# A decode step's last product: two column groups in two PSUM banks, copied by two engines, with the residual added by matmul

## The chip, the core and the metric

The kernel runs on one core of a Trainium2 chip. The metric is the device time of one launch in microseconds (us), the median of several runs. One further execution was recorded by the hardware profiler; its views are quoted here. PE is TensorE, PEld its weight loads, DVE VectorE, ACT ScalarE, POOL GpSimd and SP SyncE. L548 is line 548 of the kernel before.

## The reference

A decode step of one transformer block, batch 4, one new token, width 1024, bf16 inputs:

```python
x = A_x                                            # 4 x 1 x 1024
h = x + attention(layernorm(x), k_cache, v_cache, wq, wo)
#   q = layernorm(x) @ wq: 32 heads of 128; 4 KV heads; the last 2048 of 8192 cached rows
#   scores = q k^T * 128**-0.5; softmax; times v; @ wo (4096 x 1024)
h2 = h + (silu(n @ w1) * (n @ w3)) @ w2            # n = layernorm(h); w1, w3: 1024 x 3584; w2: 3584 x 1024
return h2                                          # 4 x 1 x 1024, bf16
```

## The kernel before

All weights and the used part of the caches pass once through one large SBUF buffer, `ring`, of five units. SP issues these loads in a fixed order (`load`, L123): wq in three pieces, K by batch entry, V, then wo, w1, w3, and w2 in five pieces of 13, 8, 4, 2 and 1 rows of 128 x 1024 (`W2B`, L114). A load waits until the part of the ring that it overwrites has been read. The order of instructions on each engine is that of the program (`manual_schedule`, L130).

The four batch entries are padded to 32 rows (R = 32), so a product of 4 x 1024 takes four column groups of the PE array: group c writes the PSUM partitions 32c to 32c+31 and holds columns 256c to 256c+255 (DQ = 256, C = 4). The stage that matters is the last:

- `h1` (L479) holds x + attention in float32, 128 x 256, in that layout of four groups.
- `hg_T` (L519) is the transposed product of silu(gate) and up, the stationary operand of the last product.
- The first two pieces of w2 (21 rows) go into `early_ps` (L533), two column groups of 512 columns each, 64 partitions by two banks. VectorE adds `early_ps` into `h1` (L544), half by half.
- The last three pieces (4, 2 and 1 rows) go into `y2_ps`, a part of the PSUM tile `small` (L548): for each row four matmuls of 256 columns, one in each of the four column groups, all in one bank.
- VectorE adds `h1` to `y2_ps` and writes `res` as bf16 (L558). Four stores of 4 rows by 512 bytes take it to the output: two on SP's queue, two on ACT's (L562).

`layernorm_T` (L187) and `up_projection` (L487) come ahead of this; the pieces of w2 are issued at L508 while the gate is computed. ACT's last work before the stores is the exponential of the gate and an addition (L511, L512). `ident_f` (L149) is a float32 identity of 128 x 128.

Of the kernel before, what the change touches and what calls it, by code (L numbers as in the profile page):

```python
# [10 lines left out]
P = 128  # L11
ACT = mybir.ActivationFunctionType
ALU = mybir.AluOpType
AX = mybir.AxisListType
BF16 = mybir.dt.bfloat16
FP32 = mybir.dt.float32
# [5 lines left out]
def kernel(  # L22
# [20 lines left out]
    nc = tc.nc  # L43

    B, _, D = A_x.shape
# [7 lines left out]
    FC = F // P  # L53
    NK = W // P
    C = 4
    R = 32
    S = R // B
    DQ = D // C
# [7 lines left out]
    x_flat = A_x.flatten_outer_dims()  # L66
    out_flat = out.flatten_outer_dims()
# [16 lines left out]
    const = ctx.enter_context(tc.tile_pool(name="const", bufs=1))  # L84
    act = ctx.enter_context(tc.tile_pool(name="act", bufs=1))
# [3 lines left out]
    ps = ctx.enter_context(tc.tile_pool(name="ps", bufs=1, space=bass.MemoryType.PSUM))  # L89
# [33 lines left out]
    def load(dst, src):  # L123
        nc.sync.dma_start(out=dst, in_=src)
# [6 lines left out]


    x_nat = act.tile([P, DQ], BF16)
    nc.gpsimd.memset(x_nat[:], 0.0)
    nc.scalar.dma_start(out=x_nat[::S, :], in_=x_flat.rearrange("b (c n) -> c b n", c=C))
    for r in (slice(0, 1), slice(1, KC // 2), slice(KC // 2, KC)):
        load(wq_s[:, r, :], wq_v[:, r, :])
    for b in range(B):
# [10 lines left out]
    ident_f = const.tile([P, P], FP32)  # L149
# [8 lines left out]
        out=same[:], in_=t32[:].rearrange("p (o h) -> p o h", o=1).to_broadcast([P, C, R])  # L158
    )
    gmask = const.tile([P, 1, Hkv], BF16)  # L160
    with nc.allow_low_precision("sums of zeros and a single one"):
        nc.vector.tensor_reduce(
            out=gmask[:, 0], in_=t32[:].rearrange("p (g r) -> p g r", g=Hkv), axis=AX.X, op=ALU.add
# [3 lines left out]
    for j in range(JM):  # L167
# [3 lines left out]
        out=nscale[:], in_=ident_f[:2, :2], scalar=-qscale, op=ALU.mult  # L171
# [5 lines left out]
        out=place[:, : R * C].rearrange("p (h e) -> p h e", e=C)[:, :, C - 1], in_=t32[:]  # L177
# [6 lines left out]
        out=gather[:, :, :B], in_=ident[:].rearrange("p (c b s) -> p c b s", c=C, b=B)[:, :, :, 0]  # L184
# [44 lines left out]
    for kc in range(KC):  # L229
        for hf in range(2):  # L230
            for c in range(C):
# [3 lines left out]
                    lhsT=xn_T[:, kc, :],  # L235
                    rhs=wq_s[:, kc, o : o + HALF * Dh],
                    start=(kc == 0),
                    stop=(kc == KC - 1),
                    tile_position=(0, R * c),
# [5 lines left out]
    for r in range(REP):  # L245
# [8 lines left out]
        out=Qm[:].rearrange("p b (g y) -> p b g y", y=QW)[:, :, :, :REP],  # L254
        in_=qT_ps[:, :, :, :B].rearrange("p r g b -> p b g r"),
# [72 lines left out]
    def softmax(b):  # L328

        p1 = act.tile([P, W // C], BF16, tag=("hg", "eg")[b % 2], name="p1")  # L330
        nc.scalar.activation(  # L331
            out=p1[:],
            in_=sc_ps[b // 2][:, b % 2],
            func=ACT.Exp,
            bias=stage[("bias", b // 2)][:, b % 2 : b % 2 + 1],
            scale=qscale,
            accum_out=rs[:, b : b + 1],
        )
        stage[("p1", b)] = p1

    def spread(b):

        P4 = ktpool.tile([P, JR * L5, Hkv], BF16, tag="P4")
        nc.vector.tensor_tensor(  # L344
            out=P4[:],
            in0=stage.pop(("p1", b))[:].rearrange("p (x o) -> p x o", o=1).to_broadcast([P, JR * L5, Hkv]),
            in1=gmask[:].to_broadcast([P, JR * L5, Hkv]),
            op=ALU.mult,
        )
        stage[("P4", b)] = P4  # L350
# [13 lines left out]
    def transpose_p(b):  # L364
        PT = ptpool.tile([P, JR, R], BF16, tag="PT")
        nc.vector.transpose(  # L366
            out=PT[:].rearrange("p j h -> p (j h)"),
            in_=stage.pop(("P4", b))[:].rearrange("p x g -> p (x g)"),
        )
        stage[("PT", b)] = PT  # L370


    def output(b):
        PT = stage.pop(("PT", b))
        o_ps = (
            small[:, 0].rearrange("p (j d) -> p j d", j=JM)
            if b % 2
            else ps.tile([P, JM, Dh], FP32, tag="ktA", name="o_ps")[:]
        )
        for i in range(JR // JM):  # L380
            nc.tensor.matmul(  # L381
                o_ps,
                lhsT=PT[:, i * JM : (i + 1) * JM, :].rearrange("p j h -> p (j h)"),
                rhs=v_s[b][:, i * JM : (i + 1) * JM, :],
                start=(i == 0),
                stop=(i == JR // JM - 1),
            )
        od = act.tile([P, JM, Dh], FP32, tag="od", bufs=1)
        nc.vector.scalar_tensor_tensor(  # L389
            out=od[:],  # L390
            in0=o_ps,
            scalar=rinv[:, b : b + 1],
            in1=jmask[:].to_broadcast([P, JM, Dh]),
            op0=ALU.mult,
            op1=ALU.mult,
        )
        o2 = act.tile([P, 2, Dh], FP32, tag="o2", bufs=1)
        nc.gpsimd.tensor_tensor(out=o2[:], in0=od[:, :2], in1=od[:, 2:], op=ALU.add)  # L398
        nc.gpsimd.tensor_tensor(out=om[:, b], in0=o2[:, 0], in1=o2[:, 1], op=ALU.add)
# [10 lines left out]
    small = ps.tile([P, 2, 512], FP32, tag="ktB")  # L410
# [11 lines left out]
    bias_of(1)  # L422
    softmax(2)
    softmax(3)
    spread(1)
    transpose_p(1)
    total(0)
# [2 lines left out]
    transpose_p(2)  # L430
    output(1)
    load(w1_s, w1_v)
    spread(3)
    transpose_p(3)
    total(1)
# [4 lines left out]
    for e in range(C):  # L440
        nc.tensor.matmul(
            on_ps[:],
            lhsT=place[:, C - 1 - e : C - 1 - e + P],
            rhs=om[:, :, e * T : (e + 1) * T],
            start=(e == 0),
            stop=(e == C - 1),
# [6 lines left out]
    for i in range(2):  # L453
        for k in range(2):
            c = i + 2 * k
            nc.tensor.matmul(
                y_ps[R * i : R * i + R, k],
                lhsT=gather[:, c, :],
                rhs=x_nat[:],
                start=(k == 0),  # L460
                stop=False,
                tile_position=(0, R * i),
                skip_group_check=True,
            )
    for t in range(T):
        row = wo_s[:, t].rearrange("p (k i n) -> p i k n", k=2, i=2)
        for i in range(2):
            nc.tensor.matmul(  # L468
                y_ps[R * i : R * i + R],
                lhsT=oP[:, t, :],  # L470
                rhs=row[:, i],
                start=False,
                stop=(t == T - 1),
                tile_position=(0, R * i),
                skip_group_check=True,
            )
    load(w3_s, w3_v)
    load(w2_s[0], w2_v[:, : W2B[0], :])
    h1 = act.tile([P, DQ], FP32)  # L479
    for k in range(2):  # L480
        nc.vector.tensor_copy(out=h1[2 * R * k : 2 * R * k + 2 * R, :], in_=y_ps[:, k])
# [25 lines left out]
    fc = W2B[0]  # L507
    for w, n in zip(w2_s[1:], W2B[1:]):  # L508
# [8 lines left out]
        out=hg[:].rearrange("p (a f) -> p a f", a=2), in0=up_ps[:, :, :FH], in1=eg[:], op=ALU.mult  # L517
    )
    hg_T = act.tile([P, FC, R], BF16)  # L519
# [1 line left out]


    early_ps = ps.tile([2 * R, 2, DQ], FP32, tag="ktA", name="early_ps")
    y2_ps = small[:, 0, :DQ]
    NE = 2
    FE = sum(W2B[:NE])

    fc = 0
    for w, n in zip(w2_s[:NE], W2B[:NE]):
        for ff in range(n):  # L530
            row = w[:, ff].rearrange("p (k i n) -> p i k n", k=2, i=2)
            for i in range(2):
                nc.tensor.matmul(  # L533
                    early_ps[R * i : R * i + R],
                    lhsT=hg_T[:, fc, :],
                    rhs=row[:, i],
                    start=(fc == 0),
                    stop=(fc == FE - 1),
                    tile_position=(0, R * i),
                )  # L540
            fc += 1
    for k in range(2):
        part = h1[2 * R * k : 2 * R * k + 2 * R, :]
        nc.vector.tensor_tensor(out=part, in0=early_ps[:, k], in1=part, op=ALU.add)  # L544
    for w, n in zip(w2_s[NE:], W2B[NE:]):
        for ff in range(n):
            for c in range(C):
                nc.tensor.matmul(  # L548
                    y2_ps[R * c : R * c + R, :],
                    lhsT=hg_T[:, fc, :],  # L550
                    rhs=w[:, ff, c * DQ : (c + 1) * DQ],
                    start=(fc == FE),
                    stop=(fc == FC - 1),
                    tile_position=(0, R * c),
                )
            fc += 1
    res = act.tile([P, DQ], BF16)
    nc.vector.tensor_tensor(out=res[:], in0=y2_ps[:], in1=h1[:], op=ALU.add)  # L558
    for i in range(2):
        for half, eng in enumerate((nc.sync, nc.scalar)):  # L560
            c = 2 * half + i
            eng.dma_start(  # L562
                out=out_flat[:, c * DQ : (c + 1) * DQ], in_=res[R * c : R * c + B, :]
            )


# [28 lines left out]
```

## Time and profile before

| what | us |
|---|---|
| median of 3 runs (139.0 to 139.16) | 139.06 |
| the profiled execution's own time | 139.25 |
| its span, first to last instruction | 137.2 |
| PE busy in the span | 75.5 |
| VectorE busy | 49.3 |
| ACT busy | 28.5 |
| GpSimd busy | 15.3 |
| DMA share of the chain that ended last | 60% |
| moved from HBM | 55.58 MB, 405 GB/s over the span |

The profile gives for each engine when it was busy, what ended its idle time, and the chain of work that ended last: from the last instruction back to whatever released it. A time in the timeline is counted from the span's start. A row of the timeline reads: start, length, engine, line, operation, what it writes and reads, how often, and in brackets the idle time before it with what ended it. A matmul's row is longer than the distance between two matmuls, since they are pipelined. A DMA row on a queue is the issue alone, not the transfer. The trace also holds the time at which each DMA engine reports its part of a transfer (a landing); 16 engines carry a large transfer.

### The profile page before, as it was taken

Reading aid. Unit: us, or ns where it says so; the run is one execution under the profiler, and the core shown is the slowest. Engines: PE = TensorE matmul, PEld = TensorE weight load, DVE = VectorE, ACT = ScalarE, POOL = GpSimd, SP = SyncE. Lnnn points to the kernel's source line nnn. Section 1 sums busy time; section 2 is a strip of 40 time slices with the busy share of each in tenths; the row PEclk is TensorE's granted clock in tenths of the full one; section 3 lists DMA queues with packets and bytes.
Section 4 is the critical chain, followed back from the end, with each engine's and each line's share of the span. In section 5 each row is a group of like instructions: output and inputs, shape, how many; then the busy total and the mean of one; then the engine's idle time right before and its main releaser. Section 6 shows DMA issues by size and latency. Waiting matters only on the chain.

```text
span 137.2 us, 1720 instructions
## 1 busy us (share of the span) xinstructions
PE 75.5 (55%) x744; PEld 41.4 (30%) x746; DVE 49.3 (36%) x47; ACT 28.5 (21%) x31; POOL 15.3 (11%) x41
## 2 busy tenths in 40 slices
PE   0002904689999983149938757971098000927450
PEld 0001301289875940033414314420043000404120
DVE  0012000016733563899699620023000297061021
ACT  3005000208949494022000000005001700000000
POOL 7304100000000000000358321002000000000000
PEclk9999995559999999555999999998556855699998
DMA  4999998999999999998979989969989899999950
GB/s 162 488 424 456 449 401 373 406 435 439 411 435 444 416 425 415 430 578 358 573 306 420 497 358 439 535 284 518 418 384 523 351 451 386 419 410 418 402 195 2
DMA packets 2795, 55.70 MB, mean 406 GB/s; under 512 B 324, under 2 KB 356, under 8 KB 612
## 3 DMA queue, kind: packets, MB, share of 16 engines
q1 hardware_dynamic: 2752, 55.58, 95.0%
q8 instruction: 6, 0.10, 0.3%
q10 hardware_dynamic: 36, 0.01, 0.0%
q14 instruction: 1, 0.01, 0.0%
HBM read 55.58 MB, written 0.01 MB: 405 GB/s over the span
## 4 chain that ended last, share of the span: by engine, by line
DMA 60%; PE 27%; DVE 6%; ACT 3%; issue 1%; SPq 1%; DVEq 0%
DMA ring<-in_B_w_dram 45%; DMA ring<-in_A_wq_dram 15%; PE kt_ps L267 9%; PE sc_ps L290 5%; PE o_ps L381 4%; PE gate L492 3%; PE q_ps L233 3%; DVE P L344 2%; DVE PT L366 2%; ACT ring L271 1%; PE small L381 1%; DVE ring L269 1%; DVE rmax L302 1%; PE qT_ps L246 1%; ACT q_sb L243 1%
## 5 line engine op out<-in xcount | busy, mean ns | idle before, releaser
L271 ACT COPY ring<-kt_ps 128x2048 bf16<-128x2048 bf16 x8 | 14.6, 1866 | 8.3 <-PE kt_ps L267 8.3
L267 PE MATMUL kt_ps<-ident,ring 128*128 128x128 bf16 x256 | 15.8, 225 | 0.6 <-DVE Qm L253 0.5
L267 PEld LDWEIGHTS <-ring 128*128 128x128 bf16 x256 | 15.3, 101 | 2.6 <-DMA ring<-in_A_k_cache_dram 1.7
L398 POOL TENSOR_TENSOR o<-od 128x256 f32<-128x256 f32 x4 | 6.8, 1696 | 59.7 <-DVE od L389 59.7
L269 DVE COPY ring<-kt_ps 128x2048 bf16<-128x2048 bf16 x8 | 9.8, 1225 | 10.1 <-PE kt_ps L267 10.1
L492 PEld LDWEIGHTS <-n_T 128*32 128x32 bf16 x128 | 4.7, 133 | 21.9 <-DMA ring<-in_B_w_dram 11.5
L233 PE MATMUL q_ps<-ring,n_T 128*32 128x512 bf16 x64 | 7.2, 627 | 7.2 <-DMA ring<-in_A_wq_dram 5.5
L513 DVE RECIPROCAL eg<-eg 128x896 f32<-128x896 f32 x1 | 5.8, 5753 | 13.2 <-ACT eg L512 13.2
L492 PE MATMUL up<-ring,n_T 128*32 128x448 bf16 x64 | 4.5, 452 | 10.8 <-DMA ring<-in_B_w_dram 10.8
L381 PEld LDWEIGHTS <-PT 128*128 128x128 bf16 x64 | 6.7, 108 | 9.2 <-issue 2.1
L344 DVE TENSOR_TENSOR P<-p,gmask 128x2048 bf16<-128x2048 bf16 x4 | 9.1, 2277 | 0.8 <-ACT p L331 0.8
L366 DVE STREAM_TRANSPOSE PT<-P 128x2048 bf16<-128x2048 bf16 x4 | 9.2, 2306 | 0.1
L492 PE MATMUL gate<-ring,n_T 128*32 128x448 bf16 x64 | 6.1, 574 | 5.5 <-DMA ring<-in_B_w_dram 5.5
L381 PE MATMUL o_ps<-ring,PT 128*128 128x512 bf16 x31 | 8.6, 431 | 0.2 <-issue 0.2
L193 PE MATMUL sums_ps<-both,mean_f 128*128 128x64 f32 x4 | 1.1, 367 | 13.0 <-ACT both L191 13.0
L290 PE MATMUL sc_ps<-ring,Qm 128*32 128x512 bf16 x64 | 7.6, 604 | 0.4 <-DVE ring L269 0.4
L533 PE MATMUL early_ps<-ring,hg_T 128*32 128x512 bf16 x42 | 4.9, 379 | 5.3 <-DMA ring<-in_B_w_dram 5.3
L381 PE MATMUL small<-ring,PT 128*128 128x512 bf16 x31 | 7.2, 379 | 0.7 <-DVE rinv L362 0.7
L468 PE MATMUL y_ps<-ring,oP 128*32 128x512 bf16 x64 | 7.1, 379 | 0.1
L233 PEld LDWEIGHTS <-n_T 128*32 128x32 bf16 x64 | 2.4, 139 | 11.2 <-issue 9.3
L253 DVE COPY Qm<-qT_ps 128x128 bf16<-128x128 bf16 x1 | 0.3, 292 | 15.0 <-PE qT_ps L246 15.0
L193 PEld LDWEIGHTS sums_ps<-both,mean_f 128*128 128x128 f32 x4 | 0.8, 250 | 13.5 <-issue 11.0
(77 smaller groups left out, 58.8 us busy)
## 6 DMA issues: line engine op xcount, KB each, us to landing
ring<-in_B_w_dram SPq DMA_DIRECT2D x2, 7168.0 KB
ring<-in_A_k_cache_dram SPq DMA_DIRECT2D x4, 2048.0 KB
ring<-in_A_v_cache_dram SPq DMA_DIRECT2D x4, 2048.0 KB, 43.0
ring<-in_A_wq_dram SPq DMA_DIRECT2D x1, 4096.0 KB, 20.7
ring<-in_B_w_dram SPq DMA_DIRECT2D x1, 3328.0 KB
ring<-in_A_wq_dram SPq DMA_DIRECT2D x1, 3072.0 KB, 11.5
ring<-in_B_w_dram SPq DMA_DIRECT2D x1, 2048.0 KB, 27.2
ring<-in_A_wq_dram SPq DMA_DIRECT2D x1, 1024.0 KB, 4.6
```

What stands on the lines that cost most here:

```text
L233: nc.tensor.matmul(q_ps[R * c : R * c + R, hf], lhsT=xn_T[:, kc, :], rhs=wq_s[:, kc, o : o + HALF * Dh], start=(kc == 0), stop=(kc == KC - 1),
L267: nc.tensor.transpose(out=kt_ps[:, jj], in_=blocks[:, jj, :], identity=ident[:])
L269: nc.vector.tensor_copy(out=blocks, in_=kt_ps[:])
L271: nc.scalar.copy(out=blocks, in_=kt_ps[:])
L290: nc.tensor.matmul(sc_ps[b // 2][R * q : R * q + R, b % 2], lhsT=Qm[:, b, g * R : (g + 1) * R], rhs=kT[:, b, g, q], start=(g == 0), stop=( ...
L344: nc.vector.tensor_tensor(out=P4[:], in0=stage.pop(("p1", b))[:].rearrange("p (x o) -> p x o", o=1).to_broadcast([P, JR * L5, Hkv]), in1=g ...
L366: nc.vector.transpose(out=PT[:].rearrange("p j h -> p (j h)"), in_=stage.pop(("P4", b))[:].rearrange("p x g -> p (x g)"),)
L381: nc.tensor.matmul(o_ps, lhsT=PT[:, i * JM : (i + 1) * JM, :].rearrange("p j h -> p (j h)"), rhs=v_s[b][:, i * JM : (i + 1) * JM, :], star ...
L398: nc.gpsimd.tensor_tensor(out=o2[:], in0=od[:, :2], in1=od[:, 2:], op=ALU.add)
L468: nc.tensor.matmul(y_ps[R * i : R * i + R], lhsT=oP[:, t, :], rhs=row[:, i], start=False, stop=(t == T - 1), tile_position=(0, R * i), ski ...
L492: nc.tensor.matmul(out_ps[R * c : R * c + R, hf, :FH], lhsT=hn_T[:, kc, :], rhs=w[:, kc, o : o + FH], start=(kc == 0), stop=(kc == KC - 1) ...
L513: nc.vector.reciprocal(out=eg[:], in_=eg[:])
```

## The change

- The last product writes two PSUM tiles, `y2_ps[0]` and `y2_ps[1]`, each of 64 partitions by 256 columns in a bank of its own (the tags that gate and up had), in two column groups. The tile k holds columns 256(2i + k) in group i. Each row of weights still takes four matmuls of 256 columns.
- The residual is no longer added by VectorE at the end. Between the piece of four rows and the piece of two, two float32 matmuls add `h1` into the two tiles. Their stationary operand is `pick`, a 128 x 2 x 64 selection that GpSimd copies from `ident_f`.
- VectorE copies `y2_ps[0]` and ACT copies `y2_ps[1]` into `res`, now 64 x 2 x 256 in bf16.
- Two stores instead of four: each has 4 rows of 1 KB, one on SP's queue and one on ACT's.
- Six loads on ACT's queue read the first 2n elements of the first n rows of x (taken as 32 rows of 128), n = 12, 8, 10, 6, 2 and 4, into a tile `x_few` that nothing reads. Two are issued behind the softmax of the last batch entry (the first of them ahead of `spread(1)`, the second behind the load of w1, in the program's order), three behind the output projection, one behind the load of the first piece of w2.

```diff
+    x_few = act.tile([16, 6, 32], BF16)
+    x_rows = x_flat.rearrange("b (r n) -> (b r) n", n=128)
+    def load_few(i, n):
+        nc.scalar.dma_start(out=x_few[:n, i, : 2 * n], in_=x_rows[:n, : 2 * n])
...
     softmax(3)
+    load_few(0, 12)
...
     load(w1_s, w1_v)
+    load_few(1, 8)
...
+    for i, n in ((2, 10), (3, 6), (4, 2)):
+        load_few(i, n)
     load(w3_s, w3_v)
     load(w2_s[0], w2_v[:, : W2B[0], :])
+    load_few(5, 4)
...
-    y2_ps = small[:, 0, :DQ]
+    y2_ps = [
+        ps.tile([2 * R, DQ], FP32, tag=tag, name="y2_ps")[:] for tag in ("scA", "scB")
+    ]
+    pick = const.tile([P, 2, 2 * R], FP32)
+    nc.gpsimd.tensor_copy(
+        out=pick[:].rearrange("p k (i s) -> p k i s", i=2),
+        in_=ident_f[:].rearrange("p (i k s) -> p k i s", i=2, k=2),
+    )
...
     for w, n in zip(w2_s[NE:], W2B[NE:]):
+        if n == 2:
+            for k in range(2):
+                nc.tensor.matmul(y2_ps[k], lhsT=pick[:, k], rhs=h1[:],
+                    start=False, stop=False, skip_group_check=True)
         for ff in range(n):
-            for c in range(C):
-                nc.tensor.matmul(
-                    y2_ps[R * c : R * c + R, :],
-                    lhsT=hg_T[:, fc, :],
-                    rhs=w[:, ff, c * DQ : (c + 1) * DQ],
-                    start=(fc == FE), stop=(fc == FC - 1),
-                    tile_position=(0, R * c),
-                )
+            for k in range(2):
+                for i in range(2):
+                    c = 2 * i + k
+                    nc.tensor.matmul(
+                        y2_ps[k][R * i : R * i + R],
+                        lhsT=hg_T[:, fc, :],
+                        rhs=w[:, ff, c * DQ : (c + 1) * DQ],
+                        start=(fc == FE), stop=(fc == FC - 1),
+                        tile_position=(0, R * i), skip_group_check=True,
+                    )
             fc += 1
-    res = act.tile([P, DQ], BF16)
-    nc.vector.tensor_tensor(out=res[:], in0=y2_ps[:], in1=h1[:], op=ALU.add)
-    for i in range(2):
-        for half, eng in enumerate((nc.sync, nc.scalar)):
-            c = 2 * half + i
-            eng.dma_start(
-                out=out_flat[:, c * DQ : (c + 1) * DQ], in_=res[R * c : R * c + B, :]
-            )
+    res = act.tile([2 * R, 2, DQ], BF16)
+    nc.vector.tensor_copy(out=res[:, 0], in_=y2_ps[0])
+    nc.scalar.copy(out=res[:, 1], in_=y2_ps[1])
+    for i, eng in enumerate((nc.sync, nc.scalar)):
+        eng.dma_start(
+            out=out_flat[:, i * 2 * DQ : (i + 1) * 2 * DQ],
+            in_=res[R * i : R * i + B].rearrange("p k n -> p (k n)"),
+        )
```

More of the change, by code (lines that the diff above doesn't have):

```diff
@@ L545 @@
     for w, n in zip(w2_s[NE:], W2B[NE:]):
-        for ff in range(n):
-            for c in range(C):
-                nc.tensor.matmul(
-                    y2_ps[R * c : R * c + R, :],
-                    lhsT=hg_T[:, fc, :],
-                    rhs=w[:, ff, c * DQ : (c + 1) * DQ],
-                    start=(fc == FE),
-                    stop=(fc == FC - 1),
-                    tile_position=(0, R * c),
-                )
-            fc += 1
-    res = act.tile([P, DQ], BF16)
-    nc.vector.tensor_tensor(out=res[:], in0=y2_ps[:], in1=h1[:], op=ALU.add)
-    for i in range(2):
-        for half, eng in enumerate((nc.sync, nc.scalar)):
-            c = 2 * half + i
-            eng.dma_start(
-                out=out_flat[:, c * DQ : (c + 1) * DQ], in_=res[R * c : R * c + B, :]
-            )
+        if n == 2:
+            for k in range(2):
+                nc.tensor.matmul(
+                    y2_ps[k],
+                    lhsT=pick[:, k],
+                    rhs=h1[:],
+                    start=False,
+                    stop=False,
+                    skip_group_check=True,
+                )
+        for ff in range(n):
+            for k in range(2):
+                for i in range(2):
+                    c = 2 * i + k
+                    nc.tensor.matmul(
+                        y2_ps[k][R * i : R * i + R],
+                        lhsT=hg_T[:, fc, :],
+                        rhs=w[:, ff, c * DQ : (c + 1) * DQ],
+                        start=(fc == FE),
+                        stop=(fc == FC - 1),
+                        tile_position=(0, R * i),
+                        skip_group_check=True,
+                    )
+            fc += 1
+    res = act.tile([2 * R, 2, DQ], BF16)
[5 more added lines that the diff above has]
+            in_=res[R * i : R * i + B].rearrange("p k n -> p (k n)"),
+        )
 _INS = ['A_x', 'A_k_cache', 'A_v_cache', 'A_wq', 'A_wo', 'B_x', 'B_w1', 'B_w3', 'B_w2']
```

## The prediction

> **What bounds the kernel now.** I read the chain that ended last first, then the page's slices, then the tail row by row. The chain's head line says what the time is made of:
>
> ```profile
> by line: DMA ring<-in_B_w_dram 44.7%; DMA ring<-in_A_wq_dram 15.1%; PE kt_ps L267 9.5%; PE sc_ps L290 5.4%; PE o_ps L381 3.5%; PE gate L492 2.8%; PE q_ps L233 2.6%; DVE P L344 1.7%; DVE PT L366 1.6%; ACT ring L271 1.4%; PE small L381 1.3%;
> ...
> 103.72 30.02 DMA ring<-in_B_w_dram
> 133.75 0.04 issue
> 133.79 0.32 PE small L548 x4
> 134.11 0.02 issue
> 134.13 0.42 DVE res L558
> ```
>
> The last 30 us of work before 133.75 us are one stream of weights; only 3.5 us come after it. The slices agree: the DMA engines are 90% busy or more in most slices up to there, then idle.
>
> ```profile
> DMA  4999998999999999998979989969989899999950
> ```
>
> So edits ahead of 131 us are worth nothing unless they move the stream, and edits behind it count in full. The timeline of the tail:
>
> ```profile
> 129.35 1.90 PE L533 MATMUL early_ps<-ring,hg_T 128*32 128x512 bf16 x16 [1.91 <-DMA ring<-in_B_w_dram]
> ...
> 131.29 0.85 DVE L544 TENSOR_TENSOR h<-early_ps,h 64x256 f32<-64x256 f32 x2 [7.38 <-PE early_ps L533]
> 131.86 0.62 PE L548 MATMUL small<-ring,hg_T 128*32 128x256 bf16 x16 [0.61 <-DMA ring<-in_B_w_dram]
> ...
> 133.13 0.40 PE L548 MATMUL small<-ring,hg_T 128*32 128x256 bf16 x8 [0.65 <-DMA ring<-in_B_w_dram]
> ...
> 133.79 0.29 PE L548 MATMUL small<-ring,hg_T 128*32 128x256 bf16 x4 [0.26 <-DMA ring<-in_B_w_dram]
> ...
> 134.13 0.42 DVE L558 TENSOR_TENSOR res<-small,h 128x256 bf16<-128x256 f32 x1 [1.99 <-PE small L548]
> 134.58 0.66 SPq L562 DMA_DIRECT2D out_dram<-res  x2
> 134.59 0.65 ACTq L562 DMA_DIRECT2D out_dram<-res  x2
> ```
>
> PE waits for each of the last three pieces of w2 (131.82, 133.09, 133.75 by their landings), and each wait leaves it idle: 0.65 us before the piece of two, 0.26 us before the last. Each queue then issues two stores. By the trace's landing events the first on ACT is complete at 135.97, its second at 136.33; SP's are complete 0.18 us before those. The kernel ends at 137.23.
>
> **The base.** The profiled execution took 139.25 us, its span 137.23, so 2.03 us lie around it; the median of the runs is 139.06. I sum differences against the profiled tail and put them on the median.
>
> **The change part by part.**
>
> *Two column groups.* Each of the seven rows of weights still takes four matmuls of 256 columns, but two column groups stand side by side instead of four. L533 is the row for two: 16 matmuls of 512 columns in 1.90 us, (1.90 - 0.38) / 7 = 0.217 us a pair, so 0.108 for a pair of 256. A row of weights costs two pairs, 0.217 us, where L548's four abreast cost (0.62 - 0.27) / 3 = 0.117. The piece of four rows then streams from 131.86 to 132.72, inside the wait for the next piece; the last row ends 0.11 us later than before, on the path.
>
> *Residual by matmul.* It stands on PE between the piece of four and the piece of two, and queued behind it are the last 12 matmuls. Its input h1 is ready (L544 ends at 132.14). An fp32 matmul shows as two passes in the trace (L441: four matmuls, x8). So two matmuls of 256 columns are four passes. The nearest row is
>
> ```profile
> 83.08 1.16 PE L441 MATMUL on_ps<-om,place 128*128 128x128 f32 x8 [2.31 <-POOL om L399]
> ```
>
> whose passes of 128 columns start 0.112 us apart after the first two. If a pass goes by its columns, one of 256 costs 0.22 and the residual 0.87. That row has 128-wide fp32 weight loads, which start 0.11 us apart as well, so the loads could be what spaces it; then a pass could cost as little as a bf16 one of 256 columns, 0.11, and the residual 0.44. I take 0.87, since L304, with two-column weights, also shows 0.11 to 0.13 between passes of 128 columns; below 0.44 nothing in the trace speaks for. The Trainium skill (FP8 and Floating Point Precision, TensorE Precision Notes) has true FP32 as four passes through the array, which at this row's bf16 pace would be an estimate of 0.87 too; no row here separates the passes.
>
> *Switch of width.* The residual writes 64 partitions, its neighbours 32 each. Where the trace goes from 128-wide to 32-wide matmuls, the next one starts late: 0.149 us after the last transpose at 42.40 instead of 0.056, 0.205 after L441 instead of 0.112, so 0.09 each time. From 32-wide to the two-column L304 there is no such loss. I take 0.09 on each side; the ends are 0 and 0.09.
>
> Sum on PE: 132.72 + 0.09 + 0.87 + 0.09 = 133.77, while the piece of two landed at 133.09. The wait that I said covers the residual (0.65 us, of which the slower piece of four has already taken a part) is too short by 0.64. Then four pairs, 0.43, to 134.20, where the last piece has landed as well; its second pair starts at 134.31 and ends 0.28 later: 134.59, against 134.08 before. **+0.51.**
>
> *Two copies for one addition.* VectorE copies bank 0 (64x256 in 0.42, L481) from 134.53 to 134.95. ACT copies bank 1: L448 takes 0.27 for 128 columns and L243 1.01 for 1024, so 0.37 for 256, from 134.64 to 135.01. No table load: the earlier copies (L448, L190) have none ahead of them. Before, the addition took 0.42. ACT is idle from 109 us on. **-0.05**, and both stores now wait for the later of two engines.
>
> *One store a queue.* Issued at 135.05, the rows of 1 KB complete 1.39 us later, as ACT's store of 512 B rows does now (134.94 to 136.33): 136.44. The second issue, 0.36 us behind the first, is gone. Last landing 136.44 against 136.33, **+0.11 in all so far** (0.51 - 0.05 - 0.36 + 0.01 of rounding).
>
> *Six small loads.* All stand on ACT. Two are issued behind L331 (63.8 us; ACT is then idle to 84.3), four behind L448 (84.6; idle to 93.3); at 0.30 an issue (L562 on ACT) that is 0.6 and 1.2 us inside gaps of 20 and 8.7. Nobody reads them. They share the DMA engines with the stream. x_nat's load put five packets on each of four engines (27 ns each, 9 the last) and left no late group in the wq landings, all within 0.41 us: at most 0.08 a packet. A load of n rows may give n engines a row and a counter update; the most loaded engine gets 12 packets: 0.11 to 0.22 us by the rows, 0.96 by the bound. In w3's landings 11 engines are done at 114.6 to 115.0 and five at 116.1 to 116.5, so most have 1.2 us of slack; I take **+0.05**.
>
> They have a second effect. The trace's transfers use eight completion counters in rotation. At the end SP waits for them two at a time, at 135.290, 135.986, 136.054, 136.346, 136.408, with a last wait at 136.473: a step that finds its counters done takes 0.065. The stores now hold the fifth to the eighth counter, and the last wait that blocks is the fourth. With six loads more and two stores fewer, the stores are transfers 27 and 28, on the third and fourth counter of the rotation, which are the first wait's pair. Three more steps then follow the landing: 3 x 0.065 = **+0.20**. In the rotation no load of weights comes to wait for a late one: each waits for the transfer eight before it, landed long ago.
>
> *Off the path.* pick is a GpSimd copy of 128x128 behind L208; GpSimd is then idle, and L211's result has 3.8 us to spare before the gate matmuls. The new banks are those of gate and up, last read at 116 and 122.2. Both cost nothing; if VectorE were slowed by the copy, the 3.8 us would still cover it.
>
> Sum: 0.11 + 0.05 + 0.20 = +0.36, so 139.06 + 0.36 = **139.4 us**.
>
> **The rivals.**
>
> 1. *The residual fits into its wait.* With passes of 0.11 and no switches PE is free at 132.72 + 0.44 = 133.16, the piece of two runs to 133.59, the last piece decides again: 133.79 + 0.11 + 0.28 = 134.18 at the end of PE, copies to 134.60, stores at 134.64, landing 136.03, 0.30 early. With +0.20 and +0.05 that is -0.05: 139.0. For it: the L441 spacing is also that of its loads. Against it: L304.
> 2. *Faster: one store round instead of two, with nothing given back.* As 1, and SP's last waits come in an order in which the stores' counters block late, as now: -0.30 from the landing, a step of 0.065 less: 138.7. It decides where the residual costs under 0.5 us and the waits' order follows the counters' use. Against it: the first wait's pair stands there in the trace of before.
> 3. *The small loads hold a late engine.* The landing of the last piece goes by the five late engines; at 0.08 a packet and 12 packets the stream ends up to 0.96 later: 140.0 to 140.4. Against it: the packets' own 9 to 27 ns.
> 4. *The copies don't run side by side,* though the change says so: they share the tile res. Then 0.37 more: 139.8. The Trainium skill (PSUM — Partial Sum Buffer, Specifications (TRN2)) lets ScalarE and VectorE read PSUM in parallel where the banks differ; no row here shows two such reads at the tail.
>
> **How the numbers follow.** The forecast has 0.55, rival 1 0.22, rival 2 0.15, rival 3 0.05, rival 4 0.03. The bound of 0.2% is 0.28 us, about what a measurement of this kernel can tell from no change. The forecast's unknowns (switches 0 to 0.18, loads 0 to 0.2, last waits) leave a fifth of it under 0.28: 0.44 slower, 0.11 the same. Slower: 0.44 + 0.08 = 0.52; same: 0.11 + 0.22 = 0.33; faster: 0.15. The range goes from 138.8, which leaves out the lower part of rival 2, to 139.9, which leaves out rival 3 and a little of the forecast. The forecast's own range is 139.2 to 139.6.
>
> **What would show it.** In the profile after: the piece of four 0.25 to 0.3 longer; four fp32 passes behind it, 0.22 apart; no wait for DMA before the last two pieces; PE done 0.5 later than the stream's last landing allowed before; ACT's copy ending last; one store a queue, 1.4 us to landing; some 1.1 us from there to the end, where it was 0.9. If PE still waits for the piece of two, the residual's price was wrong; if the w2 landings move by over 0.2, the small loads' was.

## The result: 0.6% slower

| | before | after |
|---|---|---|
| median of 6 runs of each | 139.13 us (139.0 to 139.28) | 139.98 us (139.71 to 140.25) |
| ratio | | 1.0058, interval 1.0043 to 1.0074 |
| the profiled execution | 139.25 us | 139.71 us |
| its span | 137.23 us | 137.54 us |

The direction is the one forecast, the size is not: 0.81 us (0.58%) where 0.36 was summed, and the median lies just above the range. A ratio here, with its 95% interval, is worked out from the single runs, without three that were slowed as a whole, and so can differ a little from that of the medians.

The profiled execution after is the quickest of its runs: its piece of four rows of w2 landed at 131.54, before's at 131.82. So I compare from that landing on. From it to the end of the span, the kernel before takes 5.41 us and the kernel after 6.00.

The timeline of after from the piece of four on, the weight loads left out:

```profile
131.33 0.85 DVE L561 TENSOR_TENSOR h<-early_ps,h 64x256 f32<-64x256 f32 x2 [6.44 <-PE early_ps L550]
...
131.58 1.05 PE L577 MATMUL y_ps<-ring,hg_T 128*32 128x256 bf16 x16 [0.30 <-DMA ring<-in_B_w_dram]
...
132.56 1.08 PE L565 MATMUL y_ps<-h,pick 128*64 128x256 f32 x4
...
133.57 0.83 PE L577 MATMUL y_ps<-ring,hg_T 128*32 128x256 bf16 x12
134.34 0.41 DVE L588 CAST res<-y_ps 64x256 bf16<-64x256 f32 x1 [2.16 <-PE y_ps L577]
134.44 0.37 ACT L589 CAST res<-y_ps 64x256 bf16<-64x256 f32 x1 [26.12 <-PE y_ps L577]
134.84 0.35 SPq L591 DMA_DIRECT2D out_dram<-res  x1
134.84 0.28 ACTq L591 DMA_DIRECT2D out_dram<-res  x1
```

Only the first PE row has a bracket with a DMA in it. Before, each of the last three pieces ended a wait of PE; now the residual (`x4`, four passes) starts as soon as the piece of four is through, and the last 12 matmuls follow it without a pause, although their weights landed at 132.76 and 133.37. The chain that ended last says the same:

```profile
102.60 28.94 DMA ring<-in_B_w_dram
131.54 0.04 issue
131.58 1.05 PE y_ps L577 x16
132.63 1.01 PE y_ps L565 x4
133.64 0.78 PE y_ps L577 x12
134.42 0.02 issue
134.44 0.37 ACT res L589
```

Before, the stream held the end until 133.75, and 0.32 us of PE came after it. Now it holds the end until 131.54, and PE has 2.86 us of its own after that. The transfers of the last three rows have left the path.

SP's waits from 134 us on (engine, its line, what ended the waits, then total us, how many, the longest), before and then after:

```profile
SPq L590 <- DMA out_dram<-res: 0.9, 2, 0.7
SPq L590 <- PEq L590: 0.6, 2, 0.4
```

```profile
SPq L620 <- DMA out_dram<-res: 1.3, 1, 1.3
SPq L620 <- PEq L620: 0.6, 2, 0.4
```

Before, two of SP's waits are ended by stores; after, one is, and it is the first of the row. By the trace's events the last store lands at 136.45, and SP's waits then end at 136.46, 136.53, 136.59, 136.65, 136.71 and 136.78: five steps of 0.062 to 0.065 us.

From the piece of four's landing, in us (the differences are of unrounded times):

| stretch | before | after | difference | forecast |
|---|---|---|---|---|
| landing of the four rows to PE's end | 2.26 | 2.86 | +0.60 | +0.51 |
| PE's end to the last store's landing | 2.25 | 2.04 | -0.20 | -0.40 |
| last landing to the end of the span | 0.90 | 1.10 | +0.20 | +0.20 |
| execution's time less the span | 2.03 | 2.17 | +0.14 | 0 |
| small loads on the stream | | 0 (below) | 0 | +0.05 |
| sum | | | +0.74 | +0.36 |

The sum of 0.74 lies within the ratio's interval, 0.60 to 1.03 us.

### The profile page after: what moved, and what is told of

The parts are those of the page before. It is cut to its first block, busy times and chain, and to the rows that moved or that the text cites. A ratio compares the mean times of both kernels' runs of the same rounds, so it can differ in the third digit from the quotient of the medians.

```text
span 137.5 us, 1739 instructions
## 1 busy us (share of the span) xinstructions
PE 79.5 (58%) x748; PEld 41.9 (30%) x750; DVE 49.3 (36%) x47; ACT 28.9 (21%) x32; POOL 15.5 (11%) x42
## 4 chain that ended last, share of the span: by engine, by line
DMA 69%; PE 19%; DVE 6%; SPq 2%; ACT 1%; issue 1%
DMA ring<-in_B_w_dram 44%; DMA ring<-in_A_k_cache_dram 25%; PE kt_ps L272 5%; PE sc_ps L295 4%; PE o_ps L386 3%; PE gate L502 2%; SPq L124 2%; DVE P L349 2%; DVE PT L371 2%; PE y_ps L577 1%; PE small L386 1%; DVE ring L274 1%; DVE rmax L307 1%; PE y_ps L565 1%; ACT p L336 1%
## 5 line engine op out<-in xcount | busy, mean ns | idle before, releaser
L272 PE MATMUL kt_ps<-ident,ring 128*128 128x128 bf16 x256 | 15.0, 219 | 1.3 <-DMA ring<-in_A_k_cache_dram 0.8
L272 PEld LDWEIGHTS <-ring 128*128 128x128 bf16 x256 | 14.4, 98 | 3.3 <-DMA ring<-in_A_k_cache_dram 2.7
L502 PE MATMUL up<-ring,n_T 128*32 128x448 bf16 x64 | 5.8, 548 | 11.2 <-DMA ring<-in_B_w_dram 11.2
L502 PEld LDWEIGHTS <-n_T 128*32 128x32 bf16 x128 | 5.1, 142 | 21.7 <-DMA ring<-in_B_w_dram 11.7
L475 PE MATMUL y_ps<-ring,oP 128*32 128x512 bf16 x64 | 8.8, 442 | 0.1
L502 PE MATMUL gate<-ring,n_T 128*32 128x448 bf16 x64 | 5.6, 541 | 4.4 <-DMA ring<-in_B_w_dram 4.4
L550 PE MATMUL early_ps<-ring,hg_T 128*32 128x512 bf16 x42 | 6.3, 472 | 2.9 <-DVE hg_T L223 2.9
L238 PEld LDWEIGHTS <-n_T 128*32 128x32 bf16 x64 | 2.5, 140 | 11.1 <-issue 9.2
```

What stands on the lines that cost most here:

```text
L238: nc.tensor.matmul(q_ps[R * c : R * c + R, hf], lhsT=xn_T[:, kc, :], rhs=wq_s[:, kc, o : o + HALF * Dh], start=(kc == 0), stop=(kc == KC - 1),
L272: nc.tensor.transpose(out=kt_ps[:, jj], in_=blocks[:, jj, :], identity=ident[:])
L475: nc.tensor.matmul(y_ps[R * i : R * i + R], lhsT=oP[:, t, :], rhs=row[:, i], start=False, stop=(t == T - 1), tile_position=(0, R * i), ski ...
L502: nc.tensor.matmul(out_ps[R * c : R * c + R, hf, :FH], lhsT=hn_T[:, kc, :], rhs=w[:, kc, o : o + FH], start=(kc == 0), stop=(kc == KC - 1) ...
L550: nc.tensor.matmul(early_ps[R * i : R * i + R], lhsT=hg_T[:, fc, :], rhs=row[:, i], start=(fc == 0), stop=(fc == FE - 1), tile_position=(0 ...
```

## The experiments

Each was timed beside the kernel before, whose medians were 139.26, 139.09 and 139.13 us in three rounds of experiments. "Relative to the stream" means from the landing of the piece of four to the end of the span.

**The small loads.** Twice: taken out of after (no `load_few` at all), and put alone into before.

```diff
-    load_few(0, 12)
...
-    for i, n in ((2, 10), (3, 6), (4, 2)):
-        load_few(i, n)
```

> The changed kernel without its six small loads. Theory R (the residual overflows its wait on PE, and that is most of the 0.85 us): only the place of the stores among SP's last waits changes, 0.07 to 0.13 us, so 139.9 us where the kernel before has 139.1. Theory S (the small loads cost 0.3 us or more somewhere, in the stream or outside the span): 139.6 us or less.

Measured: 140.06 us, ratio 1.0058 (1.0045 to 1.0071).

> The kernel before with the six small loads and nothing else. Theory R: 139.1 to 139.3 us, up to one or two more steps of 0.065 us behind the last landing. Theory S: 139.4 us or more, and runs that lie wider apart than those of the kernel before (139.0 to 139.3).

Measured: 139.14 us, ratio 1.0000 (0.9989 to 1.0012).

By themselves the six loads cost nothing that these intervals resolve (up to 0.17 us). In after's trace they land 7 to 17 us behind their issue, and nobody waits. What they do is move the stores' place among SP's last waits: after has 1.10 us behind the last landing, without them 1.02.

**The residual.** First it was left out of after: `h1`, which holds x, the attention and the first 21 rows of w2, is then not added.

```diff
-        if n == 2:
-            for k in range(2):
-                nc.tensor.matmul(y2_ps[k], lhsT=pick[:, k], rhs=h1[:], ...)
```

> The changed kernel without the two fp32 matmuls; its output leaves out x, the attention's part and the first two pieces of w2. Theory R: PE waits for the last two pieces of w2 again and ends some 0.5 us earlier: 139.4 us. Theory S: the matmuls weigh little on the median: 139.8 us.

Measured: 139.69 us, ratio 1.0026 (1.0015 to 1.0037). Then it was kept and moved off the path: the float32 matmuls open the two banks ahead of w2's first piece, and all five pieces go straight into these banks. VectorE's two additions of `early_ps` are gone with it.

```diff
-    early_ps = ps.tile([2 * R, 2, DQ], FP32, tag="ktA", name="early_ps")
...
+    for k in range(2):
+        nc.tensor.matmul(y2_ps[k], lhsT=pick[:, k], rhs=h1[:], start=True, stop=False, ...)
+    fc = 0
+    for w, n in zip(w2_s, W2B):
```

> All of w2 goes straight into the two banks, and the two fp32 matmuls stand ahead of the first piece of w2, where PE waits for the transposed product and the stream. VectorE's additions of the first two pieces are gone. Theory R: the same 0.5 us as without the residual, 139.4 us, the whole output computed. Theory S: 139.8 us.

Measured: 139.36 us, ratio 1.0007 (0.9997 to 1.0017). The timeline of this kernel:

```profile
121.21 1.08 PE L542 MATMUL y_ps<-h,pick 128*64 128x256 f32 x4
...
131.81 1.05 PE L556 MATMUL y_ps<-ring,hg_T 128*32 128x256 bf16 x16 [0.60 <-DMA ring<-in_B_w_dram]
...
133.02 1.02 PE L556 MATMUL y_ps<-ring,hg_T 128*32 128x256 bf16 x12 [0.16 <-DMA ring<-in_B_w_dram]
...
133.97 0.42 DVE L567 CAST res<-y_ps 64x256 bf16<-64x256 f32 x1 [9.81 <-PE y_ps L556]
134.08 0.37 ACT L568 CAST res<-y_ps 64x256 bf16<-64x256 f32 x1 [26.48 <-PE y_ps L556]
134.47 0.35 SPq L570 DMA_DIRECT2D out_dram<-res  x1
```

The residual (L542) is now computed at 121 us, and PE waits for the piece of two again, by 0.16 us. Relative to the stream this kernel takes 5.47 us, after 6.00. The difference of the two ratios is 0.0051, 0.7 us: nearly the whole loss hangs on where the residual stands. By the traces 0.59 us of it lie between the piece of four's landing and PE's end, and 0.10 outside the span. Leaving the residual out gave only 0.0032, 0.45 us, although PE ended as early. In that run the last store landed 1.83 us after its issue, where it took 1.55 with the residual moved; an instruction fetch began in between (below), which may be why.

**One store or two on a queue.** The kernel above, with its two stores of 1 KB rows cut into four of 512 bytes:

```diff
+    for k in range(2):
+        for i, eng in enumerate((nc.sync, nc.scalar)):
+            c = 2 * i + k
+            eng.dma_start(out=out_flat[:, c * DQ : (c + 1) * DQ], in_=res[R * i : R * i + B, k])
```

> The kernel with the residual ahead of the first piece (139.36 us), but with four stores of 512 B rows, two a queue, in place of two stores of 1 KB rows. SP's last waits: the last one that blocks is the third, so 0.13 us less behind the landing. Theory A (a store of 1 KB rows takes as long as one of 512 B rows, so the second issue's 0.36 us is won in full): 0.23 us more, 139.6 us. Theory B (the 1 KB rows take 0.15 to 0.25 us longer to land, and most of the gain goes there): 0 to 0.1 us more, 139.4 us.

Measured: 139.12 us against 139.09, ratio 1.0005 (0.9995 to 1.0014). From the first issue to the last landing it takes 1.79 us, with two stores 1.55. But the first two of the four stores need VectorE's copy alone and are issued earlier; from PE's end to the last landing it is 2.17 against 1.97. So merging wins 0.2 us there, not the 0.36 of a second issue, and gives 0.13 back in the steps behind the landing. That is nearer to theory B; the two ratios, 1.0005 and 1.0007, do not differ.

To separate the rows' length from the number of stores I built two more forms: before with one store a queue that takes eight rows of 512 bytes, and the moved residual with rows made of two runs of 512 bytes. Both put a third dimension into the store.

```diff
+        eng.dma_start(out=out_v[2 * half : 2 * half + 2],
+            in_=res[2 * R * half : 2 * R * half + 2 * R : S, :])
```

> The kernel before with the four batch rows of the second half of the block on partitions 8 apart (32c + 8b) instead of side by side, so that one store of 8 rows of 512 B on each queue takes the result out; four column groups, VectorE's addition and one PSUM bank as before. Theory A and B both: the second issue's 0.36 us is gone, and the rows stay at 512 B: 0.25 to 0.35 us less than the kernel before, 138.95 us; if 8 rows go to two DMA engines in turn, up to 0.1 us of that is lost. A third theory, that a store's landing goes by its bytes and not by its rows' length: 139.15 us.

Measured: 139.51 us, ratio 1.0033 (1.0021 to 1.0045).

```diff
+    out_v = out_flat.rearrange("b (k i n) -> i b k n", k=2, i=2)
+        eng.dma_start(out=out_v[i], in_=res[R * i : R * i + B])
```

> The kernel with the residual ahead of the first piece (1.0007 of the kernel before), with the column blocks dealt out so that a row of a store is two runs of 512 B instead of one of 1 KB; still one store a queue and 4 KB each. If the 1 KB rows are what makes a store land 1.55 us after its issue instead of 1.39: 0.1 to 0.17 us less, ratio 0.9997. If the third dimension makes the issue slow, as with the stores of 8 rows (first packet 1.24 us after the issue instead of 0.77): 0.4 us more, ratio 1.0035.

Measured: 139.80 us, ratio 1.0050 (1.0036 to 1.0064). The eight rows missed, for a reason that no theory had; for the two runs it stood among the expectations, and they came out slower still. The issues in the timeline, of eight rows and then of two runs:

```profile
134.46 0.66 SPq L561 DMA_DIRECT2D out_dram<-res  x1
134.46 0.59 ACTq L561 DMA_DIRECT2D out_dram<-res  x1
```

```profile
134.21 0.82 SPq L571 DMA_DIRECT2D out_dram<-res  x1
134.22 0.74 ACTq L571 DMA_DIRECT2D out_dram<-res  x1
```

One such issue takes 0.59 to 0.82 us, a plain one 0.27 to 0.35. Its first packet moves 1.24 us (ACT) and 1.59 us (SP) after the issue with eight rows, 1.38 and 1.74 with two runs; after's plain stores start at 0.76 and 0.84. Counted from the first packet, the stores of two runs land after 0.50 us on both queues, those of 1 KB rows in the kernel with the residual moved after 0.61 (ACT) and 0.71 (SP). But there the packets of the two queues overlap in time and here they don't, so the rows' length is not separated.

**An instruction fetch beside the stores.** Queue q14 fetches 8 KB near the end of the kernel, and the fetch moves when VectorE's program changes. It starts at 133.37 us before and at 136.08 after, so it could have been part of the loss. To put it among before's stores, ACT takes one of VectorE's two copies into `h1`:

```diff
-    for k in range(2):
-        nc.vector.tensor_copy(out=h1[2 * R * k : 2 * R * k + 2 * R, :], in_=y_ps[:, k])
+    nc.scalar.copy(out=h1[: 2 * R, :], in_=y_ps[:, 0])
+    nc.vector.tensor_copy(out=h1[2 * R :, :], in_=y_ps[:, 1])
```

> The kernel before with one instruction fewer on VectorE: ACT makes the first half of h1's copy at 92 us, where 3.8 us are to spare. Theory F (a fetch of 8 KB of instructions, which starts 1.2 us after VectorE has reached a fixed place in its program, moves from 133.4 us into the landing of the stores, and costs there): the fetch at 135.7 us, 2.17 us outside the span where there were 2.05, the last landing 0 to 0.4 us later, so 0.13 to 0.5 us more than the kernel before (139.3). Theory N (the fetch is of no weight): the same time as before, within 0.05 us.

Measured: 140.12 us against 139.09, ratio 1.0083 (1.0068 to 1.0097). To take it away from after's stores, VectorE gets one more instruction, a `memset` of 128x1 at the start.

> The changed kernel with one more instruction on VectorE, a memset of 128 x 1 at the start that nobody waits for. Theory F: the fetch goes back ahead of the stores, to 133.4 us, 2.05 us outside the span, so 0.13 to 0.35 us less than the changed kernel: 139.65 to 139.85 us. Theory N: 140.0 us.

Measured: 139.76 us against 139.09, ratio 1.0057 (1.0042 to 1.0073). The fetch went to 119.1 us, not to the 133.4 that was expected. The DMA view from 134.55 to 136.55 us in 40 slices of 0.05 us: what moved, in before, in after, and in before with the fetch moved in:

```profile
GB/s 0 0 0 0 0 0 0 0 0 0 0 0 0 0 0 0 41 31 10 0 0 0 0 31 41 10 0 0 0 0 0 0 0 0 0 0 0 0 0 0
```

```profile
GB/s 0 0 0 0 0 0 0 0 0 0 0 0 0 0 0 0 0 0 0 0 20 21 41 21 21 21 21 0 0 0 164 0 0 0 0 0 0 0 0 0
...
q14 instruction: 1, 0.01, 1.3%
```

```profile
GB/s 0 0 0 0 0 0 0 0 0 0 0 0 0 0 0 0 51 31 0 0 0 0 10 41 10 0 0 0 164 0 0 0 0 0 0 21 0 0 0 0
...
q14 instruction: 1, 0.01, 1.1%
```

The first row shows two bursts, the two stores of each queue. In the third row the fetch (164) follows the second burst, and the last packet of each second store goes 0.34 to 0.37 us behind its start; the second stores land 2.40 and 2.54 us after their issue instead of 1.19 to 1.39. That is the whole 1.0 us, twice what was expected at most. In the second row the fetch comes behind all of the stores' packets. Moving it away leaves the ratio where it was; in the trace SP's store then lands 1.55 us after its issue instead of 1.61. So the fetch has at most some 0.06 us in this change's loss. In the runs with the residual moved it begins only after the span has ended.

**The place among the last waits.** The moved residual with only the first two small loads, so that the stores are among the last of SP's waits:

```diff
-    for i, n in ((2, 10), (3, 6), (4, 2)):
-        load_few(i, n)
...
-    load_few(5, 4)
```

> The kernel with the residual ahead of the first piece, with two of the six small loads (the first two) left. The stores are then transfers 23 and 24, on the seventh and eighth counter of the rotation, the fourth and fifth of SP's last waits, so two steps follow the landing instead of five. If these steps cost what the sum took (0.065 us each): 0.2 us less, ratio 0.9993 of the kernel before where six loads gave 1.0007. If they cost nothing: 1.0007.

Measured: 138.90 us against 139.13, ratio 0.9993 (0.9968 to 1.0017). In the trace the last landing now ends the fifth of the waits in pairs, so one step follows where there were five with six loads. The span goes on for 0.97 us after the last landing, with six loads for 1.22: four steps less. They are there in the trace; in the ratio they are not resolved.

**A version meant to beat both.** Four column groups as before, but two banks of 128 columns each, so that VectorE and ACT can copy half each; the residual ahead of the first piece, four stores, no small loads.

```diff
+            for k in range(2):
+                for c in range(C):
+                    o = c * DQ + k * DH
+                    nc.tensor.matmul(y2_ps[k][R * c : R * c + R, :], lhsT=hg_T[:, fc, :],
+                        rhs=w[:, ff, o : o + DH], start=False, stop=(fc == FC - 1), ...)
```

> A version meant to beat both: four column groups side by side as before, but two banks of 128 columns each, the residual added by fp32 matmuls ahead of the first piece, all of w2 straight into the two banks, VectorE and ACT copying 128 columns each, the four stores of before, no small loads. Where PE keeps 0.117 us for a row of weights, the end moves by the copy alone: 0.27 us for 128 columns (L448) instead of 0.425, 0.15 us less than the kernel before, ratio 0.999. If the doubled number of matmuls and weight loads costs PE up to twice the time per row, the last row takes 0.12 more: no difference.

Measured: 139.02 us against 139.13, ratio 0.9999 (0.9985 to 1.0012). Its timeline:

```profile
131.75 1.04 PE L542 MATMUL y_ps<-ring,hg_T 128*32 128x128 bf16 x32 [0.87 <-DMA ring<-in_B_w_dram]
...
134.01 0.29 DVE L553 CAST res<-y_ps 128x128 bf16<-128x128 f32 x1 [10.03 <-PE y_ps L542]
134.12 0.27 ACT L554 CAST res<-y_ps 128x128 bf16<-128x128 f32 x1 [26.69 <-PE y_ps L542]
```

The copies are shorter (0.29 and 0.27 us), but 32 matmuls of 128 columns take 1.04 us where 16 of 256 columns took 0.62 before: with half the columns the matmuls are not half as long, and PE is as slow as with two groups. No version here is faster than before beyond its interval.

## Why the prediction was right in direction and wrong in size

- **Two column groups: right.** 16 matmuls were put at 0.86 us and a switch of width at 0.09; from their first to the residual's first PE took 0.98 with the switch, 0.03 more than the 0.95 summed.
- **Residual by matmul: right, and it is the cause.** Passes of 0.22 were taken; the trace has them at 0.267, 0.216 and 0.216, and 0.309 to the next bf16 matmul, which is a pass and a switch of 0.09. In all 1.01 for a forecast 0.96. The wait that was to cover it was too short, as said, and moving it gave 0.7 us back. Rival 1, with passes of 0.11, is out. (Of the support for 0.22, L304 was read in part: its other pair of passes in the trace stands 0.167 us apart.) The pairs of bf16 matmuls of 256 columns, side by side in two column groups, start 0.11 apart, so a float32 matmul, with two recorded passes of 0.216, took the time of four pairs. The Trainium skill (FP8 and Floating Point Precision, TensorE Precision Notes) counts four passes for true FP32; these intervals agree, though the trace records two.
- **The copies: right.** VectorE from 134.34 to 134.75, ACT from 134.44 to 134.81: they overlap. Rival 4 is out. The Trainium skill (PSUM — Partial Sum Buffer, Specifications (TRN2)) lets both engines access PSUM in parallel as long as there is no bank collision; this trace agrees.
- **One store a queue: the step that failed.** The term was that "the rows of 1 KB complete 1.39 us later, as ACT's store of 512 B rows does now". That is the slower queue's time before; the quicker one, SP's, took 1.19 to 1.21. In after the slower queue, now SP's, took 1.61, 0.22 more than put, and ACT's 1.37. Without the small loads it was 1.61 on ACT and 1.39 on SP. Where no fetch is near (the residual moved, with six small loads or two, and after with the fetch moved away) it was 1.55 to 1.56 and 1.36 to 1.38. With four stores of 512-byte rows and the residual moved it was up to 1.43 and 1.24. So a store of 1 KB rows lands 0.1 to 0.2 us later than one of 512-byte rows, on the slower queue and on the quicker, and the fetch may add 0.06 in after; the forecast took a row of 512 bytes for one of 1 KB. The packets bear this out: one of 512 bytes takes 25 to 38 ns in the traces, one of 1 KB 44 to 78, and the packets of a merged pair of stores start over 0.28 us instead of 0.10. Whether it is the rows' length or the bytes in a store, no run separates. Over the stretch it is 0.20 of the missing 0.45.
- **Three more of SP's last waits: right,** +0.20 forecast and measured. Rival 2 fell on this and on the residual.
- **Small loads: 0 instead of +0.05.** Rival 3 is out: in before they changed nothing.
- **What lies around the span: a step that the sum did not have.** "2.03 us lie around it" was held constant. By the medians of the runs it is 2.04 to 2.08 in before and in seven variants of the two kernels, and 2.16 to 2.21 in after, in after without small loads, without residual, and with the fetch moved. The cause stays open; those three runs exclude these three parts, one at a time. What the four share, and no other run has, is `early_ps` with its two additions beside the two new banks; no run takes that apart. In the version with halves it is 1.92. It is 0.14 of the missing 0.45; the rest, 0.09 on PE less 0.05 for the loads and about 0.07 between the profiled executions and the runs, is small.

## What to carry to other kernels

A wait for the last transfers is no free place: work put into it must fit with all that the same change makes longer, and here 2.0 us of PE work stood against weights that landed 1.2 us apart. An operand that is known early belongs ahead of the first piece, not in the last wait: with the residual there, PE still waited 2.1 us for the weights afterwards. At the end of a kernel, take the time of a store from one with rows as long as the new ones, on the slower queue, and count how many waits still follow the landing.

## What the runs showed that I had not expected

- An 8 KB instruction fetch that began between the packets of the last stores made them land 1.0 us later, and it was moved there by giving one VectorE instruction to another engine.
- A store with a third dimension started its packets 0.5 to 0.6 us later than a plain one on ACT's queue and 0.8 to 0.9 on SP's.
